# Two layers of Fourier mixing and one-head-of-keys attention: another order of the attention step's matmuls, the out-projection in one piece, and another engine for one copy

## The chip, the core and the metric

The kernel runs on one core of a Trainium2 chip. The metric is the device time of one execution in microseconds (us). The kernel before the change takes 3773.21 us, the median of three runs that lie between 3771.49 and 3774.22. A change of under 0.2% (about 7.5 us) cannot be told from no change with such runs.

A core has several engines that run at the same time and wait for each other through semaphores. Each works through its own instructions in the order in which the program issued them. In the profile, PE is the matrix engine (TensorE) and PEld its loading of the stationary operand, DVE is VectorE, ACT is ScalarE, POOL is GpSimd, and SP only issues transfers.

## The reference

A sequence `x` of 2048 rows with 512 columns goes through four sublayers, each with a normalization of the rows ahead of it and with its input added behind it:

```python
x = x + _A_ref(_layernorm(x), ...)   # Real(DFT over rows (DFT over columns)), by matrix products
x = x + _B_ref(_layernorm(x), ...)   # attention
x = x + _A_ref(_layernorm(x), ...)
x = x + _B_ref(_layernorm(x), ...)

def _B_ref(x, wq, wk, wv, wo):       # 32 heads of 16 columns; all heads share one k and one v
    q = (x @ wq) as 32 heads
    k, v = x @ wk, x @ wv            # 2048 x 16 each
    p = softmax(q k^T * 16 ** -0.5)
    return (p v, heads side by side) @ wo
```

All inputs and the result are float32.

## The kernel before

The kernel has two layers, and each layer has a phase A (the Fourier sublayer, then q, k and v) and a phase B (attention and the out-projection `wo`). The change touches phase B alone (`phase_b`, line 833).

**Tiles and loops.** The 2048 query rows are 16 tiles of 128 (`i`, 0 to 15). Phase B runs 32 steps per tile (`s_`, 0 to 31; `n = 32 * i + s_` counts them, 512 per layer). Steps 0 to 15 treat the first 16 heads, 16 to 31 the other 16; within such a half, each step takes one of the 16 tiles of 128 keys. One step holds, on PE:

- four **scores** (`score(i, s_, j)`, line 698), each a matmul of 512 output columns that contracts only 64 of PE's 128 rows. `j % 2` tells which 64 rows: the key tile `kz_70` uses the lower half of PE's rows (group 0), `kz_71` the upper half (group 1). Scores 0 and 1 fill one buffer `x` of two PSUM banks, scores 2 and 3 the next one. When a pair is complete, ACT computes the exponentials of both with one instruction (line 701). There are two `x` buffers.
- three **maxima** (`more_max` calls `max_half`, lines 347 and 348). Softmax needs each row's maximum ahead of the exponentials. So for query tiles that come later, PE computes scores once more into a bank `y`, and DVE takes the maximum over 512 of them. There are three `y` banks, used in turn: the matmul of a maximum waits until DVE has read the maximum three places before it. These matmuls contract 64 rows too, with the row group `g` alternating from one maximum to the next.
- four matmuls of **P*V** (`pv`, line 712), for the step that lies two steps back: exponentials times v, each of 32 output columns of PE, the four side by side, all accumulating over 16 steps in the one bank `z`. A matmul with plain float32 operands counts as two in the profile, so that there it is eight.

When a half is complete, ACT copies the sums from `z` to memory (line 715), and the next half's P*V may then begin in `z`.

**What sets the order.** The order is written out by hand. At each step the program issues P*V of two steps before, then the scores with maxima between them, then whatever is listed for that step in `out_tasks` (the tile before) and `half_tasks`. `owed(n)` says how many maxima are due by step `n`: three per step, twelve ahead, and those in `o.extra`. All engines take their instructions in this order.

**The out-projection.** `o_proj` (line 767) of tile `i` is issued at the end of step 12 of tile `i + 1`: twelve matmuls with all 128 rows (lines 87 to 89) into a bank `y`, an addition by DVE (line 777) and a store. After the sixth and the twelfth matmul it issues two maxima each, which are counted in `o.extra`, so that 32 steps and one out-projection together do 100 maxima. In the first layer, DVE then works out the next normalization's statistics (lines 135 and 136 at step 14, lines 157 to 166 at step 16).

**Handing the maxima on.** At step 27, DVE gathers the next tile's maxima (`max_neg`, lines 363 to 370); at step 29, PE transposes them into a bank `y` (`max_rows`, line 376) and ACT copies them out.

Of the kernel before, what the change touches and what calls it, by code (L numbers as in the profile page):

```python
# [22 lines left out]
NT = S // P  # L23
# [24 lines left out]
def fnet_mqa_kernel(ctx: ExitStack, tc: tile.TileContext, x_in, ct, dt_, wq, wkv, wo, out):  # L48
    nc = tc.nc
# [8 lines left out]
    def slot(k, dtype=F32):  # L58
        return sb.tile([P, S], dtype, name=f"slot{k}")

    def half(k, dtype=F32):
        return sb.tile([P, D], dtype, name=f"row{k}")

    def bank(tag):
        return ps.tile([P, 512], F32, name=tag, bufs={"y": 3, "z": 1}[tag])

    def pair():
        return ps.tile([P, 2, 512], F32, name="x", bufs=2)
# [8 lines left out]
    def split_sb(raw, hi, lo, eng=None):  # L77
        nc.scalar.copy(hi, raw)  # L78
        (eng or nc.vector).tensor_sub(lo, raw, f(hi))  # L79
# [53 lines left out]
    def ln_stats(x, t):  # L133
        st = sb.tile([P, 6], F32, name="bst", bufs=2)
        nc.vector.bn_stats(st, x)
        nc.vector.bn_aggr(mv[:, t, :], st)
# [50 lines left out]
    def make_layer(L, src, mid, dst, last):  # L187
        o = Layer()
# [118 lines left out]
        def q_half_store(t0, g):  # L307
            hl = st["qs", t0, g]
            dv = qd[t0:t0 + 2].rearrange("t (h s d) (a b q) -> s h b t d a q", h=2, s=4, a=4, b=4)
            for s in range(3):  # L310
                c0 = 256 * (s % 2)
                for h in range(2):
                    nc.sync.dma_start(dv[s, h, g].rearrange("t d a q -> (d a) t q"),
                                      f(hl[64 * h:64 * h + 64, c0:c0 + 256]).rearrange("p (t q) -> p t q", t=2))
# [29 lines left out]
        def max_half(i, pr, g, kb):  # L344
            pm = bank("y")
            gs = slice(64 * g, 64 * g + KR)
            nc.tensor.matmul(pm, o.qT[i][gs, pr, :], kz[g][gs, kb * 512:kb * 512 + 512], start=True, stop=True)  # L347
            nc.vector.reduce_max(partial(i)[:, pr, g, kb:kb + 1], pm, axis=AX.X)  # L348
# [152 lines left out]
        def phase_a(extra):  # L501
# [155 lines left out]
            for k in range(12):  # L657
                more_max()
                if k == 2:
# [3 lines left out]
        units = [(0, pr, g, 3) for pr in range(HALF, NPAIR) for g in range(2)]  # L663
        units += [(i, pr, g, kb) for i in range(1, NT) for pr in range(NPAIR) for kb in range(4) for g in range(2)
                  if (i, kb) not in early]
        o.done = o.extra = 0

        def more_max():
            if o.done < len(units) and units[o.done][0] in o.loaded | {0}:
                max_half(*units[o.done])  # L670
                o.done += 1

        def owed(n):
            return min(3 * (n + 1) + 12 + o.extra, len(units)) - o.done

        def done_with(i, pr):
            return all(u[:2] > (i, pr) for u in units[o.done:])
# [3 lines left out]
        def score(i, s_, j):  # L681
            hf, c = divmod(s_, NT)
            jj, g = divmod(j, 2)
            cp = 4 * (2 * hf + jj)
            if (i, s_) not in ptiles:
                k = i * NSTEP + s_
                ptiles[i, s_] = slot((6, 7, 2)[k % 3]).rearrange("p (j n) -> p j n", j=4)
            w = j // 2
            if i == NT - 1 and jj == 1 and o.done == len(units):
                e = bank("y")  # L690
                nc.tensor.matmul(e, kz[g][64 * g:64 * g + KR, c * P:(c + 1) * P],
                                 o.qT[i][64 * g:64 * g + KR, cp:cp + 4, :], start=True, stop=True)
                nc.scalar.activation(ptiles[i, s_][:, j, :], e, AF.Exp, scale=DH ** -0.5)
                return
            first = "e" not in st
            if first:
                st["e"] = pair()
            nc.tensor.matmul(st["e"][:, g, :], kz[g][64 * g:64 * g + KR, c * P:(c + 1) * P],  # L698
                             o.qT[i][64 * g:64 * g + KR, cp:cp + 4, :], start=True, stop=True)
            if not first:  # L700
                nc.scalar.activation(ptiles[i, s_][:, 2 * w:2 * w + 2, :], st.pop("e"), AF.Exp, scale=DH ** -0.5)  # L701
# [3 lines left out]
        def pv(i, s_):  # L705
            hf, c = divmod(s_, NT)
            if c == 0:
                acc[i, hf] = bank("z")
            a = acc[i, hf]
            pt = ptiles.pop((i, s_))  # L710
            for j in range(4):
                nc.tensor.matmul(a[32 * j:32 * j + 32, :], v1[:, c, :], pt[:, j, :], start=c == 0, stop=c == NT - 1)  # L712
            if c == NT - 1:
                oa = half(hf)
                nc.scalar.copy(oa, a)  # L715
                acc[i, hf] = oa

        bt = {}
# [42 lines left out]
        def o_mm(k):  # L761
            if k == 0:
                bt["po"] = bank("y")
            ks = slice(k * P, (k + 1) * P)
            mm3(bt["po"], bt["oh"][:, ks], bt["ol"][:, ks], woh[:, k, :], wol[:, k, :], k == 0, k == NK - 1)

        def o_proj(i):
            for k in range(NK):
                o_mm(k)
                if k % 2 and i < NT - 1:  # L770
                    for _ in range(2):
                        more_max()
                        o.extra += 1
            o_add(i)

        def o_add(i):
            nc.vector.tensor_add(bt["x"], bt["po"], bt["x"])
            (nc.sync if last else nc.gpsimd).dma_start(dst[i], bt["x"])
# [29 lines left out]
        def o_stats(i):  # L808
            if not last:
                ln_stats(bt["x"], i)  # L810

        def o_rstd(i):
            if not last:
                ln_rstd(i, 1, table=False)
# [18 lines left out]
        def phase_b(nxt):  # L833
            nonlocal woh, wol, osp
            woh = slot(4, F32R).rearrange("p (k e) -> p k e", k=NK)
            wol = slot(5, F32R).rearrange("p (k e) -> p k e", k=NK)
            def wo_load(j):
                st["wo", j] = half(4 + j)
                nc.sync.dma_start(st["wo", j], wo[:, j, :])

            for j in range(NK):
                wo_load(j)
            behind = []
            for n in range(NT * NSTEP):
                i, s_ = divmod(n, NSTEP)
                if len(behind) == 2:
                    pv(*behind.pop(0))
                behind.append((i, s_))
                g = units[o.done][2] if o.done < len(units) else 1
                for j, m in ((1 - g, 1), (g, 2), (3 - g, 0), (2 + g, 1)):  # L850
                    score(i, s_, j)
                    for _ in range(m):
                        if owed(n) >= 1:
                            more_max()
                if i == 0 and 2 <= s_ <= 8 and s_ % 2 == 0:
                    q_half_store(14, s_ // 2 - 1)
                if n == 12:
                    osp = slot(3, F32R).rearrange("p (a h n) -> p a h n", a=2, h=2)
                if i == 0 and s_ in (12, 14, 16, 18):
                    j = s_ // 2 - 6  # L860
                    split_sb(st["wo", j], woh[:, j, :], wol[:, j, :], nc.gpsimd)
                if i > 0:
                    for fn in out_tasks(i - 1).get(s_, ()):
                        fn()
                if s_ == 2:
                    for j in range(2, NT):
                        if i == max(0, j - 4 if j < 13 else j - 2):
                            qT_load(j)
                for fn in half_tasks(i).get(s_, ()):
                    fn()  # L870
                for at, j, p0, np_ in ((NT - AHEAD, i, HALF, HALF), (NSTEP - AHEAD, i + 1, 0, HALF if i == NT - 2 else NPAIR)):
                    if j in (0, NT - 1) or j == i + 1 < NT:
                        if s_ == at:
                            assert done_with(j, p0 + np_ - 1)
                            max_neg(j, p0, np_)
                        if s_ == at + 2:
                            max_rows(j, p0, np_)
            if nxt is not None:
                nxt.a_start()
            for at in behind:  # L880
                pv(*at)
            return out_tasks(NT - 1)

        def half_tasks(i):
            return {
# [4 lines left out]
        def out_tasks(i):  # L890
            return {
                1: [lambda: o_store(i, 1), lambda: o_sum(i, 1), lambda: x_load(i)], 5: [lambda: o_inv(i, 1)],
                6: [lambda: o_load(i, 1)], 9: [lambda: o_scale(i, 1)], 10: [lambda: o_hi(i, 1)],
                12: [lambda: o_proj(i)], 14: [lambda: o_stats(i)], 16: [lambda: o_rstd(i)],
                25: [lambda: o_ln(i)], 26: [lambda: o_xnh(i)], 27: [lambda: o_xnl(i)],
            }

# [49 lines left out]
```

## Time and profile before

| what | us |
|---|---|
| median of three runs | 3773.21 |
| span of the profiled execution, first to last instruction | 3768.5 |
| PE busy | 3662.8 |
| DVE busy | 2804.0 |
| ACT busy | 2371.4 |
| 32 steps of phase B, second layer (2904.19 to 2977.84 us from the span's start) | 73.65 |
| the same 32 steps: PE busy, DVE busy, ACT busy | 73.35, 64.17, 63.04 |

The span is 4.7 us shorter than the median run; a forecast that is made for the span has these 4.7 us added. In a row of the profile's timeline, the first number is the start, the second the length, "x2" says that two like instructions that follow each other were merged, and the text in brackets is how long the engine had been idle and for whom. A row of the grouped view has the count, then the busy time and the mean length in nanoseconds, then the idle time ahead of the group's instructions.

### The profile page before, as it was taken

To read this page: it belongs to the slowest core of one execution; us is meant where nothing else is said; L and a number is where in the kernel's file an instruction comes from. 1 tells how busy PE (TensorE), PEld (TensorE's weight loads), DVE (VectorE), ACT (ScalarE), POOL (GpSimd) and SP (SyncE) were. 2 spreads that over 40 slices of the span, in tenths; PEclk is the share of its full clock that TensorE was granted. 3 is DMA by queue.
4 is the path that set the end of the run, shared out by engine and by line. 5 is a ranking of instruction groups with operands and counts; after the bars stand their busy time and mean duration, and the time that the engine had idled before them with its cause. 6 is when DMAs were issued, how large, how long until landed. Compare 5 with 4: busy or idle time off the path is not lost.

```text
span 3768.5 us, 56828 instructions
## 1 busy us (share of the span) xinstructions
PE 3662.8 (97%) x21826; PEld 1982.0 (53%) x21826; DVE 2804.0 (74%) x4743; ACT 2371.4 (63%) x2846; POOL 831.8 (22%) x1009
## 2 busy tenths in 40 slices
PE   8989999999999999999999999999999999999999
PEld 6777778633433333333377777785334333333433
DVE  5165978688888888888411769777888888888882
ACT  3212211588888888888933221216888888888888
POOL 5634342211111111111155343421000000000000
PEclk9999999999999999999999999999999999999999
DMA  5543332311111100110133342413111111001100
GB/s 181 122 136 103 99 97 88 98 34 37 42 35 33 50 21 21 33 49 21 41 129 103 112 126 76 123 60 99 33 49 32 35 35 44 24 21 49 33 23 25
DMA packets 204704, 242.51 MB, mean 64 GB/s; under 512 B 36880, under 2 KB 160784, under 8 KB 197264
## 3 DMA queue, kind: packets, MB, share of 16 engines
q1 hardware_dynamic: 199504, 222.08, 19.6%
q0 software_dynamic: 4864, 16.78, 1.6%
q8 instruction: 171, 2.80, 0.3%
q14 instruction: 101, 0.83, 0.1%
q10 hardware_dynamic: 64, 0.02, 0.0%
HBM read 174.58 MB, written 63.17 MB: 63 GB/s over the span
## 4 chain that ended last, share of the span: by engine, by line
PE 82%; DVE 4%; ACT 3%; issue 3%; POOL 2%; DMA 1%; SPq 0%; POOLq 0%; ACTq 0%; DVEq 0%
PE z L712 25%; PE x L698 18%; PE y L347 11%; PE y L334 6%; PE x L87 5%; PE x L89 5%; PE x L88 5%; PE y L87 3%; DVE mxp L348 3%; PE y L89 2%; PE y L88 2%; ACT slot L701 1%; POOL row L182 1%; POOL cl L79 1%; POOL slot L84 1%
## 5 line engine op out<-in xcount | busy, mean ns | idle before, releaser
L701 ACT ACTIVATE slot<-x 128x1024 f32<-128x1024 f32 x1990 | 1942.9, 1027 | 334.8 <-PE x L698 267.1
L348 DVE TENSOR_REDUCE mxp<-y 128x1 f32<-128x512 f32 x3040 | 1908.7, 684 | 280.6 <-PE y L347 228.4
L712 PE MATMUL z<-slot,v 128*32 128x512 f32 x8192 | 1096.2, 605 | 1.9 <-ACT row L715 1.9
L698 PE MATMUL x<-slot,kz 64*128 64x512 f32 x2956 | 900.4, 446 | 4.4 <-DMA slot<-mt 3.8
L698 PEld LDWEIGHTS x<-slot,kz 64*128 64x128 f32 x2956 | 375.1, 185 | 732.1 <-ACT slot L701 597.9
L347 PE MATMUL y<-kz,slot 64*128 64x512 f32 x2272 | 747.8, 436 | 4.7 <-ACT mt L378 0.7
L335 DVE TENSOR_REDUCE mxe<-y 128x1 f32<-128x512 f32 x832 | 525.2, 684 | 122.7 <-PE y L334 121.7
L87 PE MATMUL x<-ch,xnh 128*128 128x512 f32 (+1 forms) x1152 | 432.6, 376 | 12.9 <-ACT xnh L449 8.5
L89 PE MATMUL x<-ch,xnl 128*128 128x512 f32 (+1 forms) x1152 | 429.7, 373 | 1.2 <-POOL xnl L450 0.7
L88 PE MATMUL x<-cl,xnh 128*128 128x512 f32 (+1 forms) x1152 | 427.9, 371 | 0.4 <-POOL cl L79 0.4
L334 PE MATMUL y<-kz,slot 128*128 128x512 f32 (+1 forms) x1088 | 380.4, 399 | 43.6 <-DMA slot<-qd 15.3
L752 POOL TENSOR_TENSOR row<-row,row 128x256 f32<-128x256 f32 x63 | 46.2, 734 | 1679.6 <-DMA row<-rd 971.3
L347 PEld LDWEIGHTS y<-kz,slot 64*128 64x128 f32 x2272 | 359.3, 185 | 99.0 <-DVE mxp L348 29.6
L78 ACT CAST ch<-craw 128x512 fp32r<-128x512 f32 x256 | 156.4, 619 | 387.9 <-PE x L89 366.0
L79 POOL TENSOR_TENSOR cl<-craw,ch 128x512 fp32r<-128x512 f32 x236 | 307.8, 1310 | 361.4 <-ACT ch L78 295.4
L712 PEld LDWEIGHTS z<-slot,v 128*32 128x32 f32 x8192 | 163.5, 108 | 276.7 <-issue 248.6
L334 PEld LDWEIGHTS y<-kz,slot 128*128 128x128 f32 x1088 | 203.3, 190 | 106.6 <-DVE mxe L335 27.4
L87 PEld LDWEIGHTS x<-ch,xnh 128*128 128x128 f32 x1152 | 219.5, 191 | 52.9 <-ACT xnh L449 8.5
L88 PEld LDWEIGHTS x<-cl,xnh 128*128 128x128 f32 x1152 | 219.3, 190 | 43.5 <-POOL cl L79 0.7
L89 PEld LDWEIGHTS x<-ch,xnl 128*128 128x128 f32 x1152 | 218.7, 190 | 44.6 <-POOL xnl L450 4.5
L335 DVE TENSOR_REDUCE mxp<-y 128x1 f32<-128x512 f32 (+1 forms) x256 | 146.0, 619 | 126.5 <-PE y L334 125.8
L87 PE MATMUL y<-slot,slot 128*128 128x512 f32 x384 | 156.6, 408 | 8.9 <-DVE mxp L348 5.8
(144 smaller groups left out, 2837.3 us busy)
## 6 DMA issues: line engine op xcount, KB each, us to landing
craw<-ct_in SPq DMA_DIRECT2D x112, 512.0 KB
slot<-qd SPq DMA_DIRECT2D x44, 1024.0 KB
qd<-row SPq DMA_DIRECT2D x144, 128.0 KB
od<-row SPq DMA_DIRECT2D x252, 64.0 KB
row<-x_in SPq DMA_DIRECT2D x32, 256.0 KB
mid<-row POOLq DMA_DIRECT2D x32, 256.0 KB, 2.3
craw<-ct_in SPq DMA_DIRECT2D x32, 256.0 KB
row<-mid SPq DMA_DIRECT2D x32, 256.0 KB
```

Source lines behind the costliest of these rows:

```text
L78: nc.scalar.copy(hi, raw)
L79: (eng or nc.vector).tensor_sub(lo, raw, f(hi))
L87: nc.tensor.matmul(ps_, ah, bh, start=start, stop=False)
L88: nc.tensor.matmul(ps_, ah, bl, start=False, stop=False)
L89: nc.tensor.matmul(ps_, al, bh, start=False, stop=stop)
L334: nc.tensor.matmul(pm, o.qT[i][:, pr, :], kz[g][:, c0:c0 + n], start=True, stop=True)
L335: nc.vector.reduce_max(to, pm, axis=AX.X)
L347: nc.tensor.matmul(pm, o.qT[i][gs, pr, :], kz[g][gs, kb * 512:kb * 512 + 512], start=True, stop=True)
L348: nc.vector.reduce_max(partial(i)[:, pr, g, kb:kb + 1], pm, axis=AX.X)
L698: nc.tensor.matmul(st["e"][:, g, :], kz[g][64 * g:64 * g + KR, c * P:(c + 1) * P], o.qT[i][64 * g:64 * g + KR, cp:cp + 4, :], start=True, ...
L701: nc.scalar.activation(ptiles[i, s_][:, 2 * w:2 * w + 2, :], st.pop("e"), AF.Exp, scale=DH ** -0.5)
L712: nc.tensor.matmul(a[32 * j:32 * j + 32, :], v1[:, c, :], pt[:, j, :], start=c == 0, stop=c == NT - 1)
```

## The change

The line numbers of the kernel before hold in what follows, up to line 766; behind it the changed kernel's are four lower (the addition of line 777 is line 773 there).

- In a step, scores 0 and 1 are issued first, next to each other, then up to three maxima, then scores 2 and 3, and then one more maximum if one is still due.
- `owed` no longer counts `o.extra`: 25 maxima are due per eight steps, with eight ahead. So seven steps of eight do three maxima, and the eighth (`n % 8 == 7`) does four.
- `o_proj` has no maxima between its matmuls, and it is issued at the beginning of step 12, behind P*V and ahead of the scores.
- DVE copies the finished P*V sums in place of ACT.

```diff
-        o.done = o.extra = 0
+        o.done = 0
...
-            return min(3 * (n + 1) + 12 + o.extra, len(units)) - o.done
+            return min(25 * (n + 1) // 8 + 8, len(units)) - o.done
...
-                nc.scalar.copy(oa, a)
+                nc.vector.tensor_copy(oa, a)
...
         def o_proj(i):
             for k in range(NK):
                 o_mm(k)
-                if k % 2 and i < NT - 1:
-                    for _ in range(2):
-                        more_max()
-                        o.extra += 1
             o_add(i)
...
                 behind.append((i, s_))
+                if i > 0 and s_ == 12:
+                    o_proj(i - 1)
                 g = units[o.done][2] if o.done < len(units) else 1
-                for j, m in ((1 - g, 1), (g, 2), (3 - g, 0), (2 + g, 1)):
-                    score(i, s_, j)
-                    for _ in range(m):
-                        if owed(n) >= 1:
-                            more_max()
+                score(i, s_, 0)
+                score(i, s_, 1)
+                for _ in range(min(3, owed(n))):
+                    more_max()
+                score(i, s_, 3 - g)
+                score(i, s_, 2 + g)
+                if owed(n) >= 1:
+                    more_max()
...
-            return out_tasks(NT - 1)
+            return {**out_tasks(NT - 1), 12: [lambda: o_proj(NT - 1)]}
...
-                12: [lambda: o_proj(i)], 14: [lambda: o_stats(i)], 16: [lambda: o_rstd(i)],
+                14: [lambda: o_stats(i)], 16: [lambda: o_rstd(i)],
```

How the order changes is seen at three places. The first is one step on PE in the middle of the first layer. Lines 698 are scores, lines 347 the matmuls of maxima, line 712 is P*V; `kz_70` is row group 0 and `kz_71` row group 1. Before:

```order
L698 MATMUL x<-slot_6109,kz_71 128x512
L347 MATMUL y<-kz_70,xnh 128x512
L698 MATMUL x<-slot_6109,kz_70 128x512
L347 MATMUL y<-kz_71,xnh 128x512
L347 MATMUL y<-kz_70,xnh 128x512
L698 MATMUL x<-slot_6109,kz_71 128x512
L698 MATMUL x<-slot_6109,kz_70 128x512
L712 MATMUL z<-slot_7777,v_74 32x512 x4
```

The same place now, in a step with four maxima:

```order
L698 MATMUL x<-slot_6097,kz_70 128x512
L698 MATMUL x<-slot_6097,kz_71 128x512
L347 MATMUL y<-kz_71,xnh 128x512
L347 MATMUL y<-kz_70,xnh 128x512
L347 MATMUL y<-kz_71,xnh 128x512
L698 MATMUL x<-slot_6097,kz_70 128x512
L698 MATMUL x<-slot_6097,kz_71 128x512
L347 MATMUL y<-kz_70,xnh 128x512
L712 MATMUL z<-slot_7802,v_74 32x512 x4
```

The first maximum went from second place to third, behind both scores of the first pair; the fourth stands between the last score and P*V. A step with three maxima is the same without the fourth.

The second place is the out-projection on PE. Before, after its sixth matmul:

```order
L88 MATMUL y<-slot_6032,slot_6356 128x512
L89 MATMUL y<-slot_6031,slot_6356 128x512
L347 MATMUL y<-kz_71,xnl 128x512
L347 MATMUL y<-kz_70,xnl 128x512
L87 MATMUL y<-slot_6031,slot_6356 128x512
```

Now, at its beginning (its twelve matmuls follow each other, and the scores of step 12 follow them):

```order
L698 MATMUL x<-slot_6097,kz_70 128x512
L712 MATMUL z<-slot_7898,v_74 32x512 x4
L87 MATMUL y<-slot_6031,slot_6347 128x512
L88 MATMUL y<-slot_6032,slot_6347 128x512
L89 MATMUL y<-slot_6031,slot_6347 128x512
```

The pairs of maxima (`kz`) left the out-projection, which now stands directly behind P*V.

The third place is DVE in the first layer around step 16, where a half's P*V sums are complete. Line 348 reads maxima, lines 157 to 166 belong to the normalization. Before:

```order
L348 TENSOR_REDUCE mxp_10018<-y 128x1 x6
L157 TENSOR_SCALAR lnv<-mv 128x1
L165 TENSOR_SCALAR lnw<-lnv 128x1
L166 TENSOR_SCALAR rs<-lnw 128x1
L348 TENSOR_REDUCE mxp_10018<-y 128x1 x18
```

Now:

```order
L348 TENSOR_REDUCE mxp_10020<-y 128x1 x7
L157 TENSOR_SCALAR lnv<-mv 128x1
L165 TENSOR_SCALAR lnw<-lnv 128x1
L166 TENSOR_SCALAR rs<-lnw 128x1
L715 COPY row_10551<-z 128x512
L348 TENSOR_REDUCE mxp_10020<-y 128x1 x18
```

The copy of the sums stands between the maxima of two steps, behind the normalization's three instructions.

## Prediction

> **What bounds the kernel now.** I read the page first, then the timeline of one ordinary step, because phase B repeats one step 512 times per layer.
>
> ```profile
> span 3768.5 us, 56828 instructions
> PE 3662.8 (97%) x21826; PEld 1982.0 (53%) x21826; DVE 2804.0 (74%) x4743; ACT 2371.4 (63%) x2846; POOL 831.8 (22%) x1009
> ```
>
> PE is busy nearly all the time, but this busy time is modelled, so whether PE sets the pace must be seen in the step:
>
> ```profile
> 1205.37 0.49 PE L698 MATMUL x<-slot,kz 64*128 64x512 f32 x1
> 1205.37 0.72 PE L347 MATMUL y<-kz,xnl 64*128 64x512 f32 x2
> 1205.71 0.39 PE L698 MATMUL x<-slot,kz 64*128 64x512 f32 x1
> 1205.93 1.89 DVE L348 TENSOR_REDUCE mxp<-y 128x1 f32<-128x512 f32 x3 [0.23 <-PE y L347]
> 1205.94 0.39 PE L347 MATMUL y<-kz,xnl 64*128 64x512 f32 x1
> 1206.07 0.50 PE L698 MATMUL x<-slot,kz 64*128 64x512 f32 x2
> 1206.20 1.94 ACT L701 ACTIVATE slot<-x 128x1024 f32<-128x1024 f32 x2 [0.19 <-PE x L698]
> 1206.50 1.06 PE L712 MATMUL z<-slot,v 128*32 128x512 f32 x8
> 1207.49 0.49 PE L698 MATMUL x<-slot,kz 64*128 64x512 f32 x1
> ```
>
> The step lasts 2.12 (1205.37 to 1207.49). Matmuls of the two row groups run beside each other, and within a group they follow at 0, 0.34, 0.57 and 0.80: seven matmuls in four places, the fourth half empty (the last score ends at 1206.57 and is 0.39 long, so it began at 1206.18). P*V begins at 1.13 and takes 0.99. DVE idles 0.23 and ACT 0.19 per step, both for PE: PE's own chain of four places and P*V is the bound, and any wait on PE is lost time. The first two matmuls last 0.49 and the later ones 0.39: where the weights could not be loaded ahead, the load of about 0.11 shows.
>
> **What a late bank costs.** The new order makes PE wait for `y` banks, so I looked for a place where this happens already:
>
> ```profile
> 1219.00 3.70 DVE L348 TENSOR_REDUCE mxp<-y 128x1 f32<-128x512 f32 x6
> 1220.25 0.49 PE L698 MATMUL x<-slot,kz 64*128 64x512 f32 x1
> 1220.25 0.73 PE L347 MATMUL y<-kz,xnl 64*128 64x512 f32 x2
> 1220.94 0.50 PE L347 MATMUL y<-kz,xnl 64*128 64x512 f32 x1
> 1220.94 0.73 PE L698 MATMUL x<-slot,kz 64*128 64x512 f32 x2
> 1221.60 0.30 PE L376 MATMUL y<-ident,ms 128*64 128x128 f32 x1
> 1221.83 1.07 PE L712 MATMUL z<-slot,v 128*32 128x512 f32 x8
> 1222.83 0.50 PE L698 MATMUL x<-slot,kz 64*128 64x512 f32 x1
> ```
>
> The third maximum starts at 0.69 in place of 0.57 and is 0.50 long; the last score (1220.94 + 0.73 - 0.39 = 1221.28) is at 1.03, 0.23 late, not 0.12. The scores behind the waiting maximum start with it and not before: PE lets nothing pass. So a third matmul that starts at t costs t + 0.11 - 0.57 = t - 0.46. The same holds here:
>
> ```profile
> 2903.86 0.49 PE L698 MATMUL x<-xnl,kz 64*128 64x512 f32 x1
> 2905.26 0.47 PE L87 MATMUL y<-slot,slot 128*128 128x512 f32 x1 [0.21 <-DVE mxp L348]
> 2905.57 0.39 PE L88 MATMUL y<-slot,slot 128*128 128x512 f32 x1
> 2905.80 0.40 PE L89 MATMUL y<-slot,slot 128*128 128x512 f32 x1
> 2906.49 0.40 PE L89 MATMUL y<-slot,slot 128*128 128x512 f32 x1
> 2906.82 0.50 PE L347 MATMUL y<-kz,slot 64*128 64x512 f32 x2
> 2910.23 0.50 PE L698 MATMUL x<-xnl,kz 64*128 64x512 f32 x1
> 2910.54 0.68 DVE L777 TENSOR_TENSOR row<-y,row 128x512 f32<-128x512 f32 x1
> 2911.28 0.72 PE L698 MATMUL x<-xnl,kz 64*128 64x512 f32 x2
> 2912.93 0.49 PE L698 MATMUL x<-xnl,kz 64*128 64x512 f32 x1
> ```
>
> The addition of the out-projection frees its bank at 2911.22, and a maximum, with the score that is seen at 2911.28, starts 0.06 later, at 1.05. The rule gives 0.59; the step lasted 2.70, 0.58 more than 2.12. So a freed bank reaches PE after 0.06.
>
> **The change part by part.**
>
> *Fourth maximum.* It needs the bank of its own step's first maximum. That one stood in the first place and now stands in the second: it ends at 0.34 + 0.39 = 0.73, and DVE starts 0.07 later (before: 0.49 to 0.56), at 0.80. DVE's read takes 0.69, so the bank reaches PE at 0.80 + 0.69 + 0.06 = 1.55. The weight load shows (0.11), and P*V, queued behind, follows 0.33 after the last matmul (1206.18 to 1206.50): 1.55 + 0.11 + 0.32 = 1.98 in place of 1.13, so 0.85 lost. ACT's exponentials and DVE run on meanwhile but have nothing to win. Steps 7, 15, ... 479 of each layer do this, since the last maximum falls near step 483 (1520 maxima, 8 ahead, 3.125 per step): 120 x 0.85 = +102. Without the shown load it is 0.74, +89.
>
> *Third maximum.* DVE's three reads last 1.89, now from 0.80 to 2.69; PE hears at 2.75, which is 0.63 in the next step. Rule: 0.63 - 0.46 = 0.17 lost. That step then lasts 2.29, so the next one has its bank at 0.46 and loses nothing: every second step pays. After a step with four (2.97 long) the bank is at 2.75 + 0.60 - 2.97 = 0.38: nothing. So three of eight steps pay; less those that the points below count, 11 of 32: 30 tiles x 11 x 0.17 = +56. Bounds: nothing, if DVE's first read starts 0.17 sooner than I think; 24 of 32 steps, +122, if steps don't alternate.
>
> *Out-projection.* Before, the two steps around it took 2903.86 to 2912.93 = 9.07, 4.83 above two ordinary ones, with four maxima in it. Now: twelve matmuls and the change to 64 rows, 0.31 + 10 x 0.23 + 0.33 = 2.94 behind P*V. Its addition starts 0.13 into the step (last matmul at -0.33, 0.39 long, 0.07) and takes 0.68, and the third maximum needs that bank: 0.87 - 0.46 = 0.41. 3.35 against 4.83, for 14 tiles of each layer with maxima left: 28 x -1.48 = -41.
>
> *Copy of the sums.* The trace has no such copy on DVE. The nearest rows:
>
> ```profile
> L715 ACT COPY row<-z 128x512 f32<-128x512 f32 x64 | 38.0, 594 | 1.3 <-PE z L712 1.1
> L777 DVE TENSOR_TENSOR row<-y,row 128x512 f32<-128x512 f32 x32 | 21.8, 682 | 52.7 <-PE y L89 52.7
> 2918.30 1.07 PE L712 MATMUL z<-slot,v 128*32 128x512 f32 x8
> 2920.47 1.06 PE L712 MATMUL z<-slot,v 128*32 128x512 f32 x8
> 2922.75 0.64 PE L712 MATMUL z<-slot,v 128*32 128x512 f32 x4
> ```
>
> I take 0.68, since it is DVE reading 512 values of PSUM, and 0.59 as the other end. On ACT it costs the two steps 2.17 + 2.28, 0.21 over. On DVE some 0.60 more work lies between two steps' reads, of which 0.31 falls into DVE's idle time; 0.29 comes through the third bank: +0.08 per half, 60 halves, +5 (0 at 0.59). The next P*V waits for the copy until 1.23, and starts at 1.28 anyhow. The Trainium skill ("VectorE: DVE Perf Modes", the errata's cycle table) gives VectorE 120 + 512 cycles at 0.96 GHz out of PSUM, so 0.66, and ScalarE 172 + 512 at 1.2 GHz, so 0.57, an argument against the move; by it this term would be +4, and ACT's 594 ns agrees nearly.
>
> *Transposed maxima.* Line 376 waits for the first maximum's bank as well: at 1.55 in place of the 1.35 (1221.60) before, and the step's end with it. Before, the step was 2.58, 0.46 over; now 1.55 + 1.23 (1221.60 to 1222.83) = 2.78, 0.66 over: 30 x 0.20 = +6.
>
> *First layer's normalization.*
>
> ```profile
> 1192.24 0.50 PE L698 MATMUL x<-slot,kz 64*128 64x512 f32 x1
> 1194.75 0.14 DVE L157 TENSOR_SCALAR lnv<-mv 128x1 f32<-128x1 f32 x1
> 1194.75 0.49 PE L698 MATMUL x<-slot,kz 64*128 64x512 f32 x1
> 1195.11 0.15 DVE L166 TENSOR_SCALAR rs<-lnw 128x1 int32<-128x1 int32 x1
> ```
>
> Before, statistics and these 0.52 cost one step of 2.51, 0.39 over, the copy included. Now 0.52 and the copy stand between two steps' reads: DVE is late by 0.81, and P*V waits for the copy until 1.75. I reckon 0.5 more there and 0.4 for the statistics ahead of a fourth maximum, less the 0.2 that the copy no longer takes from ACT: +0.7, 14 tiles, +10.
>
> *Earlier exponentials.* The first pair of scores is complete at 0.50 in place of 0.73 or so; ACT was waiting for PE, so this gives nothing while there are maxima. In each layer's last tile, without maxima, ACT loses a copy twice: -2 in all.
>
> Sum: 102 + 56 - 41 + 5 + 6 + 10 - 2 = +136, some of it counted where steps already lose: I take +132. 3768.5 + 132 + 4.7 = **3905 us**.
>
> **The rivals.**
>
> *Only the fourth maximum pays* (DVE starts its first read early enough for the third bank): 3905 - 56 = 3849. For it: 0.17 is a difference of long sums. Against: two places agree with the rule to 0.01.
>
> *Every step with three pays* 0.17, because lateness doesn't reset: 3905 + 66 = 3971. Against: a longer step gives the bank exactly that time.
>
> *Faster: the fourth maximum costs nothing.* The fourth place in a step is half empty, and PE would fill it while four maxima leave the out-projection. This decides only if the fourth maximum finds a free bank, that is, if the bank of the step's first maximum were freed by 0.80; DVE's read starts only then. With waits at neither maximum, 3905 - 102 - 56 = 3747. The Trainium skill ("Perfetto Trace Analysis", section Identifying the Most-Contended Engine) says to improve the engine with the highest occupancy; by that rule PE's packing decides and this rival wins. The trace speaks against it: DVE, busy 1.89 of 2.12, is late by latency, not by load.
>
> *The change does nothing*, since PE could let P*V pass a waiting maximum and the rest cancels: within 0.2%. The scores held at 1220.94 speak against it.
>
> **How the numbers follow.** Forecast 0.62, with its own range 3865 to 3945; only the fourth 0.18; every step 0.10; faster 0.06; nothing 0.02; a shortfall of both waits that still ends slower 0.02. Slower (by over 0.2%, about what runs can tell) 0.92, same 0.02, faster 0.06. The range goes from 3835, below the second case, to 3950, leaving out every step and the faster one.
>
> **What would show it.** In the changed profile, steps with four maxima last 2.97, with P*V about 1.98 behind the first score and a wait of PE's loads for line 348; other steps alternate 2.12 and 2.29; the out-projection's two steps take 7.6; ACT idles more. If a four-maximum step takes 2.2 or less, the main term is wrong; if three-maximum steps stay at 2.12, the second.

## The result and the profile after

The changed kernel takes 3879.19 us (median of four runs, 3876.2 to 3880.32). The kernel before took 3773.72 beside it (four runs, 3771.49 to 3774.45). The ratio is 1.0279, with a 95% interval of 1.0264 to 1.0294: slower by 105.5 us. The prediction was 3905, with a range of 3835 to 3950. Sign and range hold, and the forecast is 26 too long.

First the page's head after the change:

```profile
span 3874.4 us, 56828 instructions
...
PE 3730.5 (96%) x21826; PEld 1943.2 (50%) x21826; DVE 2840.2 (73%) x4807; ACT 2346.2 (61%) x2782; POOL 829.9 (21%) x1009
```

The same instructions run, with 64 moved from ACT to DVE. The span grew by 105.9 (from 3768.5). PE's busy share hardly fell and PE's busy time even rose, so this line alone would not have shown where the time went. The grouped view says more. In its rows of the kernel before, the number behind the second bar is the idle time ahead of the group, and what follows it says for whom:

```profile
L348 DVE TENSOR_REDUCE mxp<-y 128x1 f32<-128x512 f32 x3040 | 1908.7, 684 | 280.6 <-PE y L347 228.4 <-PE x L698 47.0
...
L347 PEld LDWEIGHTS y<-kz,slot 64*128 64x128 f32 x2272 | 359.3, 185 | 99.0 <-DVE mxp L348 29.6 <-DVE row L777 9.1 <-issue 7.2
```

The same groups after the change, with DVE's copy:

```profile
L348 DVE TENSOR_REDUCE mxp<-y 128x1 f32<-128x512 f32 x3040 | 1906.2, 684 | 276.3 <-PE y L347 268.0
...
L347 PEld LDWEIGHTS y<-kz,slot 64*128 64x128 f32 x2272 | 293.1, 186 | 231.4 <-DVE mxp L348 206.5 <-DVE row L773 11.8 <-DVE lnv L157 3.2
...
L715 DVE COPY row<-z 128x512 f32<-128x512 f32 x64 | 43.8, 684 | 66.4 <-PE z L712 66.1
```

PE's weight loads for maxima wait 206.5 us for DVE's reads in this largest group, where they waited 29.6. DVE in turn is idle as long as before and waits for PE: the two wait for each other through three banks, and neither is full.

The timeline shows two of the new steps, one with three maxima and one with four. (Rows of SP's queue and of PE's weight loads are left out without a mark.)

```profile
3039.84 0.50 PE L698 MATMUL x<-slot,kz 64*128 64x512 f32 x2
...
3040.18 0.72 PE L347 MATMUL y<-kz,xnh 64*128 64x512 f32 x3
...
3041.06 1.06 PE L712 MATMUL z<-slot,v 128*32 128x512 f32 x8
...
3042.06 0.50 PE L698 MATMUL x<-slot,kz 64*128 64x512 f32 x2
3042.40 0.39 PE L347 MATMUL y<-kz,xnh 64*128 64x512 f32 x2
...
3042.66 1.94 ACT L701 ACTIVATE slot<-x 128x1024 f32<-128x1024 f32 x2 [0.28 <-PE x L698]
3042.82 2.48 DVE L348 TENSOR_REDUCE mxp<-y 128x1 f32<-128x512 f32 x4 [0.33 <-PE y L347]
3042.89 0.39 PE L698 MATMUL x<-slot,kz 64*128 64x512 f32 x1
3043.57 0.49 PE L347 MATMUL y<-kz,xnh 64*128 64x512 f32 x1 [0.29 <-DVE mxp L348]
3043.99 1.07 PE L712 MATMUL z<-slot,v 128*32 128x512 f32 x8
```

In the step from 3042.06, the last score begins at 0.83 and could be followed by P*V at about 1.15. The fourth maximum stands between them. It starts at 1.51 (3043.57), 0.06 after DVE's read of the step's first maximum ended (3042.82 + 0.69 = 3043.51). P*V follows at 1.93, and from P*V to P*V it is 2.93 (3041.06 to 3043.99). The step from 3039.84 lasts 2.22, and its third matmul of a maximum is the late one. It starts at 0.57, just when it would have started anyhow, but 0.49 long (3040.18 + 0.72 = 3040.90, less 0.49, is 3040.41) where it is 0.39 to 0.42 long in a step that doesn't wait. Its weight load, which PE could not do ahead, is all that this step pays.

From the starts of all 1024 P*V's in both traces, the difference in the span by kind of step is as follows, in us. "Forecast" repeats the prediction's terms.

| term | forecast | measured |
|---|---|---|
| 120 steps with four maxima | +102 | +97 (0.81 each) |
| third maximum late, and the copies of the sums | +56 +5 | +40 |
| out-projection, 28 times | -41 | -41.5 |
| transposed maxima, 30 times | +6 | +5 |
| first layer's normalization, 14 times | +10 | +10 |
| last tile of each layer | -2 | -0.6 |
| five longer first steps of tiles (2.60 to 3.70) in the kernel before, of ordinary length after | not seen | -4 |
| start, and phase A between the layers | not seen | +1 |
| sum | +136, taken as +132 | +106 |

### The profile page after: what moved, and what is told of

Its sections match the earlier page's. It is cut to its first block, busy times and chain, and to the rows that moved or that the text cites. A ratio compares the mean times of both kernels' runs of the same rounds, so it can differ in the third digit from the quotient of the medians.

```text
span 3874.4 us, 56828 instructions
## 1 busy us (share of the span) xinstructions
PE 3730.5 (96%) x21826; PEld 1943.2 (50%) x21826; DVE 2840.2 (73%) x4807; ACT 2346.2 (61%) x2782; POOL 829.9 (21%) x1009
## 4 chain that ended last, share of the span: by engine, by line
PE 43%; DVE 3%; issue 2%; POOL 1%; ACT 1%; DMA 0%; SPq 0%; POOLq 0%; ACTq 0%; DVEq 0%
PE z L712 13%; PE x L698 8%; PE y L347 6%; PE y L334 3%; PE x L87 3%; PE x L89 3%; PE x L88 3%; DVE mxp L348 2%; PE y L87 1%; PE y L89 1%; PE y L88 1%; POOL row L182 0%; POOL cl L79 0%; PE y L691 0%; POOL slot L84 0%
## 5 line engine op out<-in xcount | busy, mean ns | idle before, releaser
L698 PE MATMUL x<-slot,kz 64*128 64x512 f32 x2956 | 865.8, 460 | 2.2 <-ACT slot L701 1.4
L698 PEld LDWEIGHTS x<-slot,kz 64*128 64x128 f32 x2956 | 365.7, 184 | 645.1 <-ACT slot L701 552.8
L347 PE MATMUL y<-kz,slot 64*128 64x512 f32 x2272 | 563.9, 415 | 35.2 <-DVE mxp L348 29.7
L347 PEld LDWEIGHTS y<-kz,slot 64*128 64x128 f32 x2272 | 293.1, 186 | 231.4 <-DVE mxp L348 206.5
```

## Experiments: the parts alone

The theory was the prediction's: PE waits for banks, at the fourth maximum above all. The rivals were that only one of the waits pays, that every step pays, and that the packing of PE's places decides.

**The new order alone**, in the kernel before, with its maxima still in the out-projection and ACT copying:

```diff
-                for j, m in ((1 - g, 1), (g, 2), (3 - g, 0), (2 + g, 1)):
-                    score(i, s_, j)
-                    for _ in range(m):
-                        if owed(n) >= 1:
-                            more_max()
+                score(i, s_, 0)
+                score(i, s_, 1)
+                for _ in range(min(3, owed(n))):
+                    more_max()
+                score(i, s_, 3 - g)
+                score(i, s_, 2 + g)
+                if owed(n) >= 1:
+                    more_max()
```

> The kernel before with the new order of scores and maxima alone; three maxima per step, the extra four still in the out-projection, copies on ACT. Theory (late banks): the first maximum stands in the second place, so DVE frees the third bank late; steps alternate between 2.12 and 2.24 us as the three-maximum steps of the changed kernel do, 15 of 32 steps pay 0.12, and the transposed maxima's step is 2.74 in place of 2.58: 30 tiles x (15 x 0.12 + 0.16) = +59, about 3832 us. Rival (the pair order is free, and all of the loss comes from the steps with four maxima and what they leave behind): steps of 2.12, 3774 within 8.

Measured: 3821.38 us, ratio 1.0127 (1.0112 to 1.0142). Four P*V's in its timeline, with the copy of the sums by ACT that falls between them:

```profile
2990.30 1.07 PE L712 MATMUL z<-slot,v 128*32 128x512 f32 x8
...
2991.63 0.59 ACT L715 COPY row<-z 128x512 f32<-128x512 f32 x1
...
2992.55 1.06 PE L712 MATMUL z<-slot,v 128*32 128x512 f32 x8
...
2994.67 1.07 PE L712 MATMUL z<-slot,v 128*32 128x512 f32 x8
...
2996.91 0.64 PE L712 MATMUL z<-slot,v 128*32 128x512 f32 x4
```

The steps last 2.25, 2.12 and 2.24. They alternate, as forecast, since a step that was late gives the next one its bank earlier in the step. The rivals "nothing" and "every step pays" fall here. A late step costs 0.12, where the prediction had 0.17. So the order alone already makes this kernel slower, by 48 us.

That is 11 us less than was expected for this run, and the late steps are not the reason, since they were expected at 0.12. The main reason is the copy. The first two of the three steps above are those around ACT's copy, and they last as long as steps without a copy. Before the change such a pair took 2.17 + 2.28, 0.21 more than two ordinary steps, so that 60 x 0.21 = 13 us come back here. (The two steps around the out-projection, on the other hand, cost 0.21 more than before, 28 x 0.21 = 6 us, and 14 and not 15 steps of a tile are late.) The pairing of scores therefore does bring something back: it makes ACT's copy free.

**The fourth maximum alone**: the old order of a step, the maxima taken out of the out-projection and counted 25 per eight steps.

```diff
-        o.done = o.extra = 0
+        o.done = 0
...
-            return min(3 * (n + 1) + 12 + o.extra, len(units)) - o.done
+            return min(25 * (n + 1) // 8 + 8, len(units)) - o.done
...
-                if k % 2 and i < NT - 1:
-                    for _ in range(2):
-                        more_max()
-                        o.extra += 1
```

> The kernel before with the new count alone: 25 maxima per eight steps, none in the out-projection, which stays in one piece at the end of step 12; the old order in the step; copies on ACT. Theory (late banks): the first maximum still stands in the first place, DVE reads it from 0.56 to 1.25, the fourth gets its bank at 1.31 in place of 1.55, so a step with four lasts about 2.74 in place of 2.94: 120 x 0.62 = +74; the out-projection costs about 3.07, as in the last tile, in place of 4.83: 28 x -1.76 = -49; together +25, about 3798 us. Rival (a fourth maximum costs 0.82 wherever the first stands, because it is a fourth matmul in a full row group): +98 - 49, about 3823 us. Second rival (the half empty place takes it free): 3725 us.

Measured: 3798.84 us, ratio 1.0068 (1.0051 to 1.0085). A step with four maxima in this kernel:

```profile
2989.17 1.07 PE L712 MATMUL z<-slot,v 128*32 128x512 f32 x8
...
2990.16 0.72 PE L347 MATMUL y<-kz,xnh 64*128 64x512 f32 x2
...
2991.48 0.49 PE L347 MATMUL y<-kz,xnh 64*128 64x512 f32 x1
...
2991.90 0.64 PE L712 MATMUL z<-slot,v 128*32 128x512 f32 x4
```

Here the first maximum is in the first place, and the fourth starts at 1.32; the prediction's way of reckoning gives 0.57 + 0.69 + 0.06 = 1.32 (DVE's first read starts 0.57 into the old step). P*V to P*V takes 2.73, 0.61 more than an ordinary step. So the fourth maximum waits for its own step's first in either order, and the new order adds 0.2 by moving that first one to the second place. The out-projection without maxima is 3.2 over two ordinary steps here, against 4.85 with four of them: a maximum costs (4.85 - 3.2) / 4 = 0.41 there on average, and 0.61 at the end of a step. 120 x 0.61 - 28 x 1.65 = +27, and 25 were measured. Both rivals of this run, 3823 and 3725, fall.

**The copy alone**, in the kernel before:

```diff
-                nc.scalar.copy(oa, a)
+                nc.vector.tensor_copy(oa, a)
```

> The kernel before with the sums of P*V copied by DVE alone. Theory: in the old order DVE's slack between two steps' reads is about as large, so a copy costs 0.2 to 0.25 as it does on ACT, but in the first layer it stands behind the normalization's three instructions, and P*V waits for it: 14 x 0.5 = +7, about 3780 us. Rival (a copy on DVE costs 0.4 or more, since DVE is the engine whose lateness PE feels): 60 x 0.2 + 7 = +19 or more, 3793 us and up.

Measured: 3778.54 us, ratio 1.0014 (1.0004 to 1.0023). That is some 5 us, about as expected; the rival, 3793 and up, falls. In the profile it lies in the first layer, whose tiles are some 0.45 longer (2.29 and 2.45 for the two steps around the normalization's end), while in the second layer the two steps around a copy take 2.12 + 2.30 in place of 2.17 + 2.28.

**The copy undone**, in the changed kernel (the line above the other way round):

> The changed kernel with the sums copied by ACT again. Theory: in the new order DVE is late by itself and ACT idles, so that the move to DVE costs there what it doesn't cost in the old order: 0.27 per half becomes about 0.1, 60 x -0.17 = -10, and the 0.5 behind the normalization goes, 14 x -0.5 = -7; about 3862 us. Rival (copies cost the same on both): 3879 within 4.

Measured: 3856.67 us, ratio to the kernel before 1.022 (1.0204 to 1.0235), 22.5 below the changed kernel. The steps around a copy by ACT, with most of the rows left out:

```profile
3053.35 1.07 PE L712 MATMUL z<-slot,v 128*32 128x512 f32 x8
...
3054.35 0.50 PE L698 MATMUL x<-slot,kz 64*128 64x512 f32 x2
...
3054.65 0.59 ACT L715 COPY row<-z 128x512 f32<-128x512 f32 x1
...
3055.12 3.10 ACT L701 ACTIVATE slot<-x 128x1024 f32<-128x1024 f32 x3
...
3055.60 1.07 PE L712 MATMUL z<-slot,v 128*32 128x512 f32 x8
...
3057.71 0.64 PE L712 MATMUL z<-slot,v 128*32 128x512 f32 x4
```

And around a copy by DVE in the changed kernel:

```profile
3069.06 0.68 DVE L715 COPY row<-z 128x512 f32<-128x512 f32 x1
...
3069.66 3.26 DVE L348 TENSOR_REDUCE mxp<-y 128x1 f32<-128x512 f32 x5
...
3069.85 1.06 PE L712 MATMUL z<-slot,v 128*32 128x512 f32 x8
...
3072.25 0.64 PE L712 MATMUL z<-slot,v 128*32 128x512 f32 x4
```

With ACT's copy the two steps take 2.25 and 2.11, just the alternation of steps without any copy. With DVE's copy the steps are 2.24 and 2.40 (3069.85 to 3072.25), since DVE's reads of maxima come late through it. Over all halves that is 0.26 each, about 15 us; some 6 more lie in the first layer, where the copy stands behind the normalization's three instructions on DVE. So the same edit costs 5 us in the old order and 22.5 in the new one.

What hides ACT's copy shows beside the same place in the kernel before:

```profile
2919.30 0.50 PE L698 MATMUL x<-xnl,kz 64*128 64x512 f32 x1
...
2919.82 0.59 ACT L715 COPY row<-z 128x512 f32<-128x512 f32 x1
...
2920.29 3.03 ACT L701 ACTIVATE slot<-x 128x1024 f32<-128x1024 f32 x3
...
2922.31 0.18 PEld L698 LDWEIGHTS x<-xnl,kz 64*128 64x128 f32 x2 [0.32 <-ACT slot L701]
```

In the old order the second pair of scores of the next step waits for the exponentials that the copy has delayed. In the new order the first pair of scores is complete sooner, and the exponentials of an ordinary step begin 0.60 into it (3042.06 to 3042.66), where it was 0.83 (1205.37 to 1206.20). Behind a copy they begin 0.77 into the step (3054.35 to 3055.12) in place of 0.99, and in the next step the second pair of scores (3057.16, 0.57 into it) names no wait. No run separates this from the 0.12 by which every second step of the new order is longer, which gives ACT time too.

## Experiments: the wait at the fourth maximum

**The fourth maximum moved behind the next P*V**, in the changed kernel. Its bank's wait then stands ahead of the next step's scores in place of P*V.

```diff
+                if n and late:
+                    more_max()
                 g = units[o.done][2] if o.done < len(units) else 1
...
-                if owed(n) >= 1:
-                    more_max()
+                late = owed(n) >= 1
```

> The changed kernel with the fourth maximum issued behind the P*V that it held up, ahead of the next step's scores. Theory (three banks, not the place): the next step then has four maxima between two P*V, the last of which finds its bank only when DVE has read the first of them, at about 1.3; the loss moves by one step and stays 0.7 to 1.0, so that the total is 3879 within 20. Rival (the loss is P*V queued behind the fourth): the fourth is one more matmul, 0.23 or less, 120 x -0.6, about 3807 us.

Measured: 3860.2 us (two runs), ratio 1.0231 (1.0212 to 1.0251), 19 below the changed kernel. Its PE at such a place:

```profile
3034.54 1.06 PE L712 MATMUL z<-slot,v 128*32 128x512 f32 x8
3035.54 0.49 PE L347 MATMUL y<-kz,xnh 64*128 64x512 f32 x1
...
3036.81 0.49 PE L347 MATMUL y<-kz,xnh 64*128 64x512 f32 x1 [0.19 <-DVE mxp L348]
...
3037.47 1.07 PE L712 MATMUL z<-slot,v 128*32 128x512 f32 x8
```

The fourth maximum (3035.54) is free of waits here, and the step is 2.93 long all the same: now its third own maximum waits, for the bank that the added one has pushed it to. So it isn't that P*V stood behind the waiting matmul; in this order four maxima in a step cost about 0.8 on three banks, with the extra one ahead of P*V or behind it. The rival (3807) falls. Of the 19 us, about 16 are elsewhere: the long step now comes directly ahead of the two steps around a copy, and these take 2.12 + 2.25 in place of 2.24 + 2.39, 60 times 0.26. The rest is in the first layer, around the normalization.

**The first read of a four-maximum step made twice**, in the changed kernel. If the wait is for this read, doubling it must lengthen just these 120 steps, by one read:

```diff
-            nc.vector.reduce_max(partial(i)[:, pr, g, kb:kb + 1], pm, axis=AX.X)
+            for _ in range(2 if twice else 1):
+                nc.vector.reduce_max(partial(i)[:, pr, g, kb:kb + 1], pm, axis=AX.X)
...
-                for _ in range(min(3, owed(n))):
-                    more_max()
+                four = owed(n) == 4
+                for k in range(min(3, owed(n))):
+                    more_max(four and k == 0)
```

> The changed kernel in which DVE reads the first maximum of each step with four maxima twice, so that its bank is freed 0.60 later (the result is the same). Theory (the fourth waits for this read): these steps last 2.94 + 0.60 = 3.54, 120 x 0.60 = +72, about 3951 us. Rival (the fourth's cost is PE's own, or that of a bank that another reader frees): DVE has 0.3 to 0.8 idle in and after such a step, so that little is added, 3879 to 3890 us.

Measured: 3968.42 us (two runs), ratio 1.0518 (1.0498 to 1.0538), 89 above the changed kernel. (Line numbers in this kernel are one higher from 349 on.)

```profile
3101.70 0.50 PE L699 MATMUL x<-slot,kz 64*128 64x512 f32 x2
...
3102.47 2.61 DVE L349 TENSOR_REDUCE mxp<-y 128x1 f32<-128x512 f32 x4 [0.36 <-PE y L347]
...
3103.94 0.49 PE L347 MATMUL y<-kz,xnh 64*128 64x512 f32 x1 [1.04 <-DVE mxp L349]
...
3104.36 0.64 PE L713 MATMUL z<-slot,v 128*32 128x512 f32 x4
```

The fourth maximum starts at 2.24 in place of 1.51, and P*V stays 0.42 behind it. 120 x 0.73 = 88 of the 89 us. DVE's first read sets the end of these steps one to one, which shows the bank's wait as the cause. The step was lengthened by 0.73 and not by the 0.60 expected, of which more below.

## Experiments: a version that is faster than both

The changed kernel has one part that gains: its out-projection, which stands directly behind P*V. In the old order, with the pairs of maxima kept but issued ahead of the first and the seventh of its matmuls, it can be had alone:

```diff
             for k in range(NK):
-                o_mm(k)
-                if k % 2 and i < NT - 1:
+                if k % 2 == 0 and i < NT - 1:
                     for _ in range(2):
                         more_max()
                         o.extra += 1
+                o_mm(k)
...
+                if i > 0 and s_ == 12:
+                    o_proj(i - 1)
...
-            return out_tasks(NT - 1)
+            return {**out_tasks(NT - 1), 12: [lambda: o_proj(NT - 1)]}
...
-                12: [lambda: o_proj(i)], 14: [lambda: o_stats(i)], 16: [lambda: o_rstd(i)],
+                14: [lambda: o_stats(i)], 16: [lambda: o_rstd(i)],
```

(`NK` is 2 here: each `o_mm` is six matmuls.)

> The kernel before with the out-projection moved to the beginning of step 12, behind P*V, and its two pairs of maxima ahead of the first and the seventh matmul in place of behind the sixth and the twelfth; all else as before. Theory: the pair behind P*V finds banks at once, the out-projection's bank no longer waits 0.28, and its addition on DVE comes 0.4 sooner; from the pieces (0.43 for a pair and the change to 128 rows, twelve matmuls, 0.41 of wait for the addition's bank) the two steps cost 4.43 in place of 4.83 above two ordinary ones: 28 x -0.40 = -11, about 3762 us. Rival (each change between 64 and 128 rows costs what it costs, whatever the place): 3774 within 3.

Measured: 3763.6 us, ratio 0.9976 (0.9967 to 0.9985), 9 to 10 us below the kernel before, where 11 were expected. The out-projection is 4.42 over two ordinary steps in the second layer, as reckoned. If one without maxima costs 3.2 here too, as it does at the end of a step in the second experiment, each of its four maxima costs 0.31. The rival, no change within 3 us, falls. The out-projection's addition still stood ahead of a third maximum that waited, so in the same step one maximum was moved behind the last score:

```diff
-                for j, m in ((1 - g, 1), (g, 2), (3 - g, 0), (2 + g, 1)):
+                w = i > 0 and s_ == 12
+                for j, m in ((1 - g, 1), (g, 2 - w), (3 - g, 0), (2 + g, 1)):
```

> As the run with the out-projection ahead, and in step 12 the third maximum stands behind the last score, so that the scores don't wait for the addition's bank. Theory: the 0.41 becomes 0.17, 4.19 in place of 4.83: 28 x -0.64 = -18, about 3756 us. Rival (the maximum behind the last score holds up P*V by as much as it held up the scores): as the run with the out-projection ahead.

Measured: 3756.64 us, ratio 0.9957 (0.9944 to 0.997), faster than the kernel before by some 16 us and than the changed one by 123. PE at its out-projection, most of the matmuls left out:

```profile
2968.26 1.06 PE L712 MATMUL z<-slot,v 128*32 128x512 f32 x8
2969.26 0.49 PE L347 MATMUL y<-kz,xnh 64*128 64x512 f32 x2
2969.73 0.47 PE L87 MATMUL y<-slot,slot 128*128 128x512 f32 x1
...
2971.30 0.49 PE L347 MATMUL y<-kz,xnh 64*128 64x512 f32 x2
...
2974.16 0.50 PE L347 MATMUL y<-kz,xnh 64*128 64x512 f32 x1
2974.60 1.06 PE L712 MATMUL z<-slot,v 128*32 128x512 f32 x8
```

No row of PE names a wait for line 348 here, and P*V to P*V takes 6.34, then 2.12. The two pairs stand ahead of six matmuls of the out-projection each, in which DVE has time to read.

## Why the prediction was right, and what was mis-sized

- **Fourth maximum: mechanism and place as forecast, 0.81 in place of 0.85.** Its wait, the queued P*V and the 0.42 from its start to P*V are in the rows above, and the doubled read shows the cause. It starts at 1.51, not 1.55, since DVE starts its first read at 0.76 and not at 0.80. +97 for +102.
- **Third maximum: the term that was mis-sized.** "DVE's three reads last 1.89, now from 0.80 to 2.69": they last 1.89, but start at 0.75 to 0.77, and the bank comes back at 0.57 to 0.60 of the next step, not at 0.63. The rule t - 0.46 holds and gives 0.11 to 0.14; 0.12 was measured. The step that failed is the 0.07 from the matmul's end to DVE's start, which was read from a first matmul with its load exposed, while this one stands in the second place. A difference of long sums of 0.17 loses about a third through 0.04. The count was right: 11 steps of a tile are late. With the copies, it came to +40 for +61, the largest part of the 26 us.
- **Out-projection: right to a tenth.** On PE of the changed kernel:

```profile
3052.74 1.07 PE L712 MATMUL z<-slot,v 128*32 128x512 f32 x8
3053.73 0.50 PE L87 MATMUL y<-slot,slot 128*128 128x512 f32 x1
...
3056.68 0.50 PE L698 MATMUL x<-slot,kz 64*128 64x512 f32 x2
...
3058.19 1.06 PE L712 MATMUL z<-slot,v 128*32 128x512 f32 x8
```

  Its matmuls take 2.95 (3053.73 to 3056.68; forecast 2.94), and P*V to P*V 5.45; with the step behind it (2.12) it is 3.35 over, the forecast's 3.35.
- **Copy: the term about right, the reason against a gain from ACT wrong.** DVE's copy costs 0.26 to 0.27 per half and ACT's had cost 0.21 before, so that the two kernels differ by 60 x 0.06 or some 4 us through it, for the forecast's +5. But "earlier exponentials ... gives nothing" missed that they let ACT's own copy pass for nothing in the new order, so that the move to DVE gave up a copy that had become free. That is why undoing the move gains 22.5 us, and not 5. The duration, taken as 0.68, is 0.684. The Trainium skill ("VectorE: DVE Perf Modes", the errata section's cycle table) gives an estimate of 0.66; the measurement is 4% above it.
- **Transposed maxima, normalization, last tiles**: +14 together, for +14. The parts of the normalization's +0.7 came as forecast too: 0.35 at the fourth maximum behind the statistics and 0.55 at the copy, less 0.2 that ACT's copy no longer costs there.
- **Rivals.** "Only the fourth pays" and "every step pays" fall through the alternation of 2.12 and 2.24, seen both in the changed kernel and in the new order alone. "Faster" falls through the fourth maximum's start, 0.68 behind the place that was free for it. What remains of it is that the out-projection without maxima does gain its 41 us; the maxima cost more where they went. So PE's packing, on which the rule by occupancy put this rival, did not decide: the place was free and the bank was not. "The change does nothing" falls with the result, and P*V did not pass the waiting maximum but followed it by 0.42.

The Trainium skill ("Perfetto Trace Analysis", section Optimization Strategy) says that a gap that repeats on the engine that should be full can mean too few buffers. The trace agrees: PE's gap at the fourth maximum (0.29 in the rows above) comes back every eighth step, with three banks and four maxima. Whether a fourth bank would remove it was not tried; no run shows it.

The -4 us of five longer steps has another cause than the banks. They are first steps of tiles, and in four of the five the profile says that PE's first score waits for a transfer of the tile's transposed maxima (line 383). The longest, of 3.70:

```profile
1451.19 0.47 PE L698 MATMUL x<-slot,kz 64*128 64x512 f32 x1 [1.42 <-DMA slot<-mt]
```

The fifth names ACT. All five come back in the three other runs that keep the old order and count (the copy alone and the two with the out-projection ahead), and none in the changed kernel, whose steps between the transposition and the next tile are longer. That this gives the transfer its time is likely, but no run tests it.

## What to carry to other kernels

When producer and consumer share a few banks in turn, ask of each extra use at what time its bank was last filled and read, not whether an engine has room: here an extra matmul cost 0.31 to 0.41 beside a long block, 0.61 at the end of a step, and 0.81 when the step's first fill was moved one place back. A late bank costs the weight load even when it comes just in time. And price a move between engines in the new order, not in the old one: the same copy was worth 5 us in one order and 22.5 in the other.

## What the runs showed of the hardware

- DVE starts 0.03 after a matmul that is 0.39 long (3042.40 + 0.39 to 3042.82), and 0.07 after one that is 0.49 long with its load exposed (1205.86 to 1205.93 before the change). The ends of matmuls are modelled in the profile, so it stays open whether DVE starts sooner or the ends are drawn unevenly; the start of the read is 0.04 earlier than reckoned all the same.
- Three reads of three banks into different columns take 1.89, so each further one adds 0.60 to the first's 0.69. A second read of the same bank into the same column added 0.73: there the reads don't overlap, and about 0.04 lies between them. Whether the bank or the column is the reason wasn't tried.
- A bank that comes back just at the planned start still costs 0.10 to 0.12: the matmul's weight load begins only with the wait's end (both start at 3040.41 in the step of 2.22).
